# A one-token attention decode kernel: one head in each of six groups scored by a multiply and a reduce, the last group of heads scored on TensorE

## The chip, the cores and the metric

The kernel runs on one core of one Trainium2 chip. The metric is the device time of one execution in microseconds (us), as the median of several executions. The kernel before takes 87.77 us (median of 6 runs, 87.69 to 87.98). Profile times are of one profiled execution each, counted from the start of its span.

## The reference, cut to what matters

The input is one token (a row of 512). Attention and a feed-forward part both read its normalised form, and both are added to it.

```python
W = min(4096, max(256, Sk // 4))                      # 1024 keys of 4096
q = (x @ wq).reshape(B, Sq, 32, 128)                  # 32 heads of 128
k = k_cache[:, :, Sk - W:, :];  v = v_cache[:, :, Sk - W:, :]
scores = einsum("bhqd,bhkd->bhqk", q, k) * (128 ** -0.5)
o = einsum("bhqk,bhkd->bhqd", softmax(scores), v)
attn = o.reshape(B, Sq, 4096) @ wo
ffn  = (relu(xn @ w1 + b1) ** 2) @ w2 + b2
out  = x + attn + ffn
```

Nearly all of it is loading: 1024 keys and values of 32 heads, and four weight matrices, 27.99 MB in all.

## The kernel before

The heads are handled in eight groups of four. All large loads go through one queue, in a fixed order; five K blocks and four V blocks have room, so later ones wait until an earlier group has used its buffer.

```python
DMA_STREAM = ("wq0a", "k0", "wq0b", "wq1", "k1", "v0", "k2", "wq2", "w1", "k3", "wq3", "v1", "k4", "wo0", "v2", "k5", "w2a",
              "w2b", "wo1", "v3", "k6", "wo2", "k7", "v4", "wo3", "v5", "wo4", "v6", "wo5", "v7", "wo6", "wo7")
```

The scores of a head come from VectorE: 1024 keys lie as 128 partitions by J = 8 columns of 128 numbers. For each column, one fused instruction multiplies by the broadcast query and sums.

```python
for j in range(J):
    ins = E.tensor_tensor_reduce(
        out=ttr_views[junk_par][:, j, :], in0=KB[:, (h // G % NKSLOT) * G + h % G, j * DH:(j + 1) * DH],
        in1=qbc[:, di % NQBC, hh * DH:(hh + 1) * DH], scale=1.0, scalar=0.0,
        op0=ALU.mult, op1=ALU.add, accum_out=ScS[:, h, j:j + 1])
```

Then follow, per group, a maximum, the exponentials (ScalarE), the sum and the division (which gives `Pn`), P·V on TensorE, and the output product with `wo`, also on TensorE, summed up in one bank over all heads:

```python
for hh in range(G):                                   # emit_wo, for group g
    h = g * G + hh
    ins = E.matmul(FIN[0:1, 0:NOUT], lhsT=OTsb[:, h:h + 1], rhs=WoB[:, h, :], start=False, stop=(h == H - 1))
```

So the last thing that can happen is: the last V block (v7) and the last output weights (wo6, wo7) land, P·V of group 7, eight output matmuls, one copy, one store.

## Time and profile before

| What | Value | Where read |
|---|---|---|
| time, median | 87.77 us | the runs |
| span of the profiled execution | 85.9 us | page |
| VectorE busy | 66.5 us, 77% | page, part 1 |
| DMA engines 90% busy or more | 4 to about 75 us (the prediction read 2 to about 73) | page, part 2 |
| TensorE waits for v7 until | 78.75 us | timeline |
| ... for output weights until | 80.11 us | timeline |
| last eight output matmuls | 3.57 us | timeline |

The end of the chain of waits of the kernel before (start, us, what):

```profile
67.36 12.62 DMA WoB<-in_A_wo_dram
80.11 3.59 PE pb L770 x8
83.72 0.68 DVE finsb L806
```

Its timeline (start, us, engine, line, operation; in brackets the idle time before it and what ended that):

```profile
76.64 0.19 DVE L736 TENSOR_TENSOR Pn<-Ex,rden 128x32 bf16<-128x32 f32 x1
...
78.75 0.99 PE L752 MATMUL pb<-Pn,VB 128*128 128x1 bf16 x32 [0.57 <-DMA VB<-in_A_v_cache_dram]
...
80.11 3.57 PE L770 MATMUL pb<-WoB,OTsb 128*1 128x512 bf16 x8 [0.37 <-DMA WoB<-in_A_wo_dram]
```

Group 7's softmax is ready at 76.83 us (76.64 + 0.19). P·V then waits for the last V block until 78.75, and the output matmuls wait for their weights until 80.11. The loads end last, VectorE about 2 us before them.

The groups of VectorE's fused score instruction and its accumulator read (busy us, mean ns):

```profile
L667 DVE CUSTOM_DVE_ANT_0 ttrjunk<-KB,qbc 128x128 bf16<-128x128 bf16 x256 | 55.9, 279 | 2.6 <-ACT qbc L525 2.6
L667 DVE DVE_READ_ACCUMULATOR2_ANT ScS<- 128x1 f32 x256 | 19.3, 75 | 0.0
```

These 512 instructions are most of VectorE's 575. They overlap; in the timeline one fused instruction starts every 0.2125 us, so a head takes 8 x 0.2125 = 1.70 us.

### The profile page before, as it was taken

How to read it: one execution, taken by the hardware profiler on the slowest of the kernel's cores; microseconds unless marked ns; L12 is line 12 of the kernel's file. 1: busy time of each engine (PE TensorE's matmuls, PEld its weight loads, DVE VectorE, ACT ScalarE, POOL GpSimd, SP SyncE). 2: the span in 40 equal slices, each digit the busy share in tenths (PEclk: the TensorE clock that was granted, in tenths of full speed). 3: DMA queues.
4: the chain of work that ended last, by engine and by line, in shares of the span. 5: the costliest groups of instructions: out<-in, count | busy, mean ns of one | idle time of the engine just before them, and what ended most of it. 6: DMA issues, size and time to landing. Idle time of an engine off the chain costs nothing.

```text
span 85.9 us, 1607 instructions
## 1 busy us (share of the span) xinstructions
PE 50.1 (58%) x422; PEld 23.8 (28%) x424; DVE 66.5 (77%) x575; ACT 18.6 (22%) x84; POOL 1.5 (2%) x12
## 2 busy tenths in 40 slices
PE   0018769300269799596341119999415959677890
PEld 0002122000253395224240103245114252533210
DVE  0760799999998599999899999989999999310002
ACT  2370222205002250028006000400320060320000
POOL 6000000000000000000000000000000000000000
PEclk9999999999999999999999999999995555555555
DMA  0899999999999999999999999999999999971000
GB/s 2 293 394 372 387 387 385 386 386 391 390 387 386 381 386 387 376 368 385 385 358 344 348 379 387 370 376 388 370 381 367 379 364 383 365 246 41 15 0 0
DMA packets 17265, 28.09 MB, mean 327 GB/s; under 512 B 516, under 2 KB 7015, under 8 KB 17256
## 3 DMA queue, kind: packets, MB, share of 16 engines
q1 hardware_dynamic: 17252, 27.99, 91.6%
q8 instruction: 3, 0.05, 0.2%
q14 instruction: 6, 0.05, 0.2%
q10 hardware_dynamic: 4, 0.00, 0.0%
HBM read 27.99 MB, written 0.00 MB: 326 GB/s over the span
## 4 chain that ended last, share of the span: by engine, by line
DVE 40%; DMA 33%; PE 18%; ACT 3%; issue 3%; SPq 1%; DVEq 0%
DVE ttrjunk L667 30%; DMA VB<-in_A_v_cache_dram 17%; DMA WoB<-in_A_wo_dram 15%; PE pb L517 10%; PE pb L770 4%; PE pb L752 2%; DMA xrow<-in_A_x_dram 2%; DVE ScS L667 1%; ACT qbc L525 1%; ACT Ex L720 1%; SPq L285 1%; DVE gmx L695 1%; PE pb L688 1%; DVE finsb L806 1%; DVE st L375 1%
## 5 line engine op out<-in xcount | busy, mean ns | idle before, releaser
L667 DVE CUSTOM_DVE_ANT_0 ttrjunk<-KB,qbc 128x128 bf16<-128x128 bf16 x256 | 55.9, 279 | 2.6 <-ACT qbc L525 2.6
L667 DVE DVE_READ_ACCUMULATOR2_ANT ScS<- 128x1 f32 x256 | 19.3, 75 | 0.0
L517 PE MATMUL pb<-WqB,XnRep 128*128 128x512 bf16 x30 | 13.8, 631 | 2.8 <-DMA WqB<-in_A_wq_dram 1.4
L720 ACT ACTIVATE Ex<-ScS,nb 128x8 f32<-128x8 f32 x32 | 9.2, 289 | 25.7 <-DVE nb L710 25.7
L770 PE MATMUL pb<-WoB,OTsb 128*1 128x512 bf16 x32 | 12.1, 532 | 0.7 <-DMA WoB<-in_A_wo_dram 0.7
L752 PE MATMUL pb<-Pn,VB 128*128 128x1 bf16 x256 | 8.0, 165 | 5.1 <-DMA VB<-in_A_v_cache_dram 3.2
L752 PEld LDWEIGHTS pb<-Pn,VB 128*128 128x128 bf16 x256 | 7.4, 103 | 6.7 <-DMA VB<-in_A_v_cache_dram 2.8
L728 PE MATMUL pb<-rs,ones_f 128*128 128x4 f32 x16 | 4.5, 352 | 8.1 <-ACT Ex L720 4.8
L525 ACT ACTIVATE qbc<-pb 128x512 bf16<-128x512 f32 x8 | 4.8, 597 | 16.2 <-PE pb L517 16.2
L517 PEld LDWEIGHTS pb<-WqB,XnRep 128*128 128x128 bf16 x32 | 4.0, 137 | 10.4 <-issue 6.1
L728 PEld LDWEIGHTS pb<-rs,ones_f 128*128 128x128 f32 x16 | 3.8, 295 | 10.3 <-ACT Ex L720 5.1
L806 DVE CAST finsb<-pb 1x512 bf16<-1x512 f32 x1 | 0.7, 679 | 6.9 <-PE pb L770 6.9
L720 ACT ACTIVATION_READ_ACCUMULATOR Ex<-ScS,nb 128x1 f32 x32 | 6.0, 187 | 0.0
L704 PE MATMUL pb<-dgall,ones_bf 4*128 4x4 bf16 x8 | 1.4, 181 | 7.5 <-DVE dgall L697 7.5
L464 PE MATMUL pb<-W2B,hT 128*1 128x512 bf16 (+1 forms) x11 | 4.9, 627 | 0.0
L759 ACT ACTIVATE OTsb<-pb 128x4 bf16<-128x4 f32 x8 | 1.3, 165 | 16.3 <-PE pb L752 16.3
L688 PE MATMUL pb<-ident_bf,m 128*4 128x128 bf16 x8 | 2.1, 265 | 3.9 <-DVE m L679 3.1
L770 PEld LDWEIGHTS pb<-WoB,OTsb 128*1 128x1 bf16 x32 | 2.8, 98 | 5.7 <-issue 3.6
L704 PEld LDWEIGHTS pb<-dgall,ones_bf 4*128 4x128 bf16 x8 | 0.8, 98 | 10.5 <-DVE dgall L697 8.4
L414 PE MATMUL pb<-ones_bf,xnrow 1*128 1x1 bf16 x4 | 0.3, 165 | 5.6 <-DVE xnrow L404 5.6
L695 DVE TENSOR_REDUCE gmx<-pb 4x1 f32<-4x128 bf16 x8 | 2.2, 275 | 1.6 <-PE pb L688 1.6
L734 DVE RECIPROCAL rden<-pb 128x4 f32<-128x4 f32 x8 | 1.4, 174 | 2.2 <-PE pb L728 2.0
(45 smaller groups left out, 26.3 us busy)
## 6 DMA issues: line engine op xcount, KB each, us to landing
KB<-in_A_k_cache_dram SPq DMA_DIRECT2D x8, 1024.0 KB, 12.9
VB<-in_A_v_cache_dram SPq DMA_DIRECT2D x8, 1024.0 KB, 14.0
WoB<-in_A_wo_dram SPq DMA_DIRECT2D x8, 512.0 KB, 12.7
WqB<-in_A_wq_dram SPq DMA_DIRECT2D x3, 1024.0 KB, 15.0
W1B<-in_B_w_dram SPq DMA_DIRECT2D x1, 1376.0 KB, 15.5
W2B<-in_B_w_dram SPq DMA_DIRECT2D x1, 1280.0 KB, 12.9
WqB<-in_A_wq_dram SPq DMA_DIRECT2D x2, 512.0 KB, 5.4
W2B<-in_B_w_dram SPq DMA_DIRECT2D x1, 96.0 KB, 14.8
```

What stands on the lines that cost most here:

```text
L464: ins = E.matmul(FIN[0:1, 0:NOUT], lhsT=hT[0:cw, c:c + 1], rhs=W2B[0:cw, c, :], start=False, stop=False)
L517: ins = E.matmul(QBB[di % 2][:, 0:QBCW], lhsT=XnRep[:, kc, :], rhs=WqB[:, kc, g * QBCW:(g + 1) * QBCW], start=(kc == 0), stop=(kc == KC - 1))
L525: return K.E.activation(out=qbc[:, di % NQBC, :], in_=QBB[di % 2][:, 0:QBCW], func=ACT.Copy)
L667: ins = E.tensor_tensor_reduce(out=ttr_views[junk_par][:, j, :], in0=KB[:, (h // G % NKSLOT) * G + h % G, j * DH:(j + 1) * DH], in1=qbc[:, ...
L688: return K.E.matmul(hlpbf[0:G, TB_C0:TB_C0 + P], lhsT=m1[:, gs], rhs=ident_bf[:, :], start=True, stop=True, is_transpose=True)
L695: i1 = E.tensor_reduce(out=gmx[0:G, g:g + 1], in_=hlpbf[0:G, TB_C0:TB_C0 + P], axis=AX.X, op=ALU.max)
L704: return K.E.matmul(hlp[:, B_C0:B_C0 + G], lhsT=ones_bf[0:G, :], rhs=dgall[0:G, g, :], start=True, stop=True)
L720: ins = E.activation(out=Ex[:, h, :], in_=srcs[hh], func=ACT.Exp, bias=nb[:, h:h + 1], scale=SCALE, accum_out=rs[:, h:h + 1])
L728: return K.E.matmul(hlp[:, D_C0:D_C0 + G], lhsT=ones_f[:, :], rhs=rs[:, gs], start=True, stop=True)
L752: ins = E.matmul(hlp[:, OT_C0 + hh:OT_C0 + hh + 1], lhsT=VB[:, vh, j * DH:(j + 1) * DH], rhs=Pn[:, h, j:j + 1], start=(j == 0), stop=(j == ...
L770: ins = E.matmul(FIN[0:1, 0:NOUT], lhsT=OTsb[:, h:h + 1], rhs=WoB[:, h, :], start=False, stop=(h == H - 1))
L806: return K.E.tensor_copy(out=finsb[0:1, :], in_=FIN[0:1, 0:NOUT])
```

## The change

The intent is to relieve VectorE. In groups 0 to 5 one head each (3, 7, 11, 15, 19, 23) is scored by one multiply over all 1024 elements and one reduce, instead of eight fused instructions. Group 7's four heads are scored on TensorE: K is transposed there, ScalarE copies it out of PSUM, and TensorE multiplies it with the query. The diff, cut to its core:

```diff
+MIXED_PE_HEADS = {7: 4}
+TT_HEADS = (3, 7, 11, 15, 19, 23)
...
+    pe_heads = [h for h in range(H) if (h % G) >= G - n_pe_in_group[h // G]]
+    dve_heads = [h for h in range(H) if (h % G) < G - n_pe_in_group[h // G]]
...
+                    if h in TT_HEADS:
+                        K.sync(E.tensor_tensor(
+                            out=ttr_views[junk_par],
+                            in0=KB[:, (h // G % NKSLOT) * G + h % G, :].rearrange("p (j d) -> p j d", j=J),
+                            in1=qbc[:, di % NQBC, hh * DH:(hh + 1) * DH].unsqueeze(1).to_broadcast([P, J, DH]),
+                            op=ALU.mult))
+                        return E.tensor_reduce(out=ScS[:, h, :], in_=ttr_views[junk_par], axis=AX.X, op=ALU.add)
...
+            for p in plist:
+                make_pair_tasks(p)          # TensorE transposes, ScalarE copies
+            sdeps = ["ktc%d" % p for p in plist] + ["qTc%d" % g] + bank_free_deps
...
```

## The prediction

> **What bounds the kernel now.** The load stream. The page's 40 slices show the 16 DMA engines at 90% or more from 2 to about 73 us, and 27.99 MB moved; the stretch table gives 360 to 388 GB/s between 9 and 75 us. The chain of waits ends: V load 51.0 to 65.2, output-weight load 67.4 to 80.0, eight output matmuls 80.1 to 83.7 (3.6 us), copy 0.68, output DMA. VectorE is 77% busy and fills 40% of the chain, but the timeline shows its last score at 72.7 and the last weights (Pn) of group 7 at 76.8, while the last V block lands at about 78.7 and the output weights at 80.0. So VectorE has about 2 us of slack. Loads are issued back to back from 20 to 71.8 us; buffers come free earlier (the last V load is issued at 65.95, its releaser ends at about 60.1).
>
> **What the change does.**
> 1. Six heads (one in each of groups 0 to 5) swap eight fused multiply-reduces, 0.2125 us apart = 1.70 us per head, for one multiply of 1024 bf16 elements and one reduce. [...] From the trace's reduce (512 bf16: 674 ns) I estimate 1.2 us for the reduce[...]. With a wait between: about 1.9 us, 0.2 us *slower* per head, about +1.2 us of VectorE in all (at worst +4.5).
> 2. Group 7 leaves VectorE: -4 x 1.70 = -6.8 us. TensorE gets 32 transposes, 32 score matmuls and 16 small query matmuls, and loses four 512-wide ones; ScalarE gets four PSUM copies of 1024 (estimated about 1 us each, from 0.60 us for 512) and loses one of 0.60.
>
> VectorE net: some 2 to 6 us less busy (66.5 to about 61-63).
>
> **How much is on the critical path.** Almost none: bytes, load order and buffers are unchanged, so the last load still lands at about 80 us, followed by the same eight matmuls, copy and store.
>
> One real chance of gain: the TensorE clock. The last eight matmuls run 0.44 us apart; six of the same shape at 57.7 us ran 0.24 us apart. The stretch table puts the clock drop near 64 us, after 3 us of little TensorE work. [...] Group 7's transposes would run at about 62 to 66, in that hole. If the clock then stays up to the end, the last eight matmuls take 1.9 instead of 3.6 us: -1.7 us. I give that one in three.
>
> **Prediction:** 87.3 us, range 86.0 to 88.2. Faster by over 2%: 0.14; within 2%: 0.80; slower: 0.06.
>
> **What would show it.** Right: DMA slices unchanged, last output weights landing at 79.5 to 80.5, chain ending in DMA then output matmuls; VectorE busy 60 to 63; pair multiply+reduce about 1.9 us; Pn of group 7 ready several us before the last V. The clock question: spacing of the last eight matmuls, 0.24 or 0.44.
>
> **What would make it wrong.** VectorE slower in groups 0 to 5, starving the load queue; the in-order TensorE or ScalarE stalling on the new transposes or copies and pushing P·V past the load end; the slow trickle of the last loads between 75 and 80 us (138 GB/s) changing in length; the clock staying up (faster).

## More of the kernel before

The page of the kernel before, parts 1 to 3 (busy time by engine; the span in 40 slices of 2.15 us; the DMA queues with packets, MB, and share of the 16 engines' time). PE is TensorE's matmuls, PEld its weight loads, DVE VectorE, ACT ScalarE, POOL GpSimd:

```profile
span 85.9 us, 1607 instructions
...
PE 50.1 (58%) x422; PEld 23.8 (28%) x424; DVE 66.5 (77%) x575; ACT 18.6 (22%) x84; POOL 1.5 (2%) x12
...
DMA  0899999999999999999999999999999999971000
GB/s 2 293 394 372 387 387 385 386 386 391 390 387 386 381 386 387 376 368 385 385 358 344 348 379 387 370 376 388 370 381 367 379 364 383 365 246 41 15 0 0
...
q1 hardware_dynamic: 17252, 27.99, 91.6%
q8 instruction: 3, 0.05, 0.2%
q14 instruction: 6, 0.05, 0.2%
```

Two things are to be seen. The load stream is full almost to the end, but it does not stop at once: after 365 GB/s come 246, 41 and 15, so a small remainder dribbles in for about 6 us. And beside the kernel's own queue (q1) there are two queues called "instruction", with nine packets in all.

## The result, and the profile after

The changed kernel takes 86.43 us (median of 7 runs, 86.18 to 86.50). Executions over 1.5% slower than the fastest of the same kernel are left out of the means. The ratio to the kernel before is 0.9848, 95% interval 0.9836 to 0.9859. (A ratio is the mean time of one kernel's fast runs over that of the other's of the same rounds, so it is not quite the ratio of the medians.) The gain of 1.3 us is within the predicted range, but nearly three times the 0.47 us that was forecast.

The same parts of the page after (slices of 2.11 us):

```profile
span 84.3 us, 1614 instructions
...
PE 51.3 (61%) x499; PEld 26.1 (31%) x500; DVE 61.1 (73%) x428; ACT 21.6 (26%) x87; POOL 1.5 (2%) x12
...
DMA  0899999999999999999999999999999999995000
GB/s 2 290 389 370 386 387 386 387 388 387 392 388 387 385 389 387 386 364 383 388 368 349 330 363 388 378 371 383 384 367 381 365 382 368 381 359 176 23 0 0
...
q1 hardware_dynamic: 17252, 27.99, 93.5%
q8 instruction: 4, 0.07, 0.3%
q14 instruction: 4, 0.03, 0.1%
```

The kernel's own loads are the same: 17252 packets, 27.99 MB. VectorE is 5.4 us less busy. The remainder at the end is shorter, and the instruction packets have changed: q14 (8 KB a packet) fell from 6 to 4, q8 (16 KB a packet) rose from 3 to 4. TensorE's program grew from 870 to 1023 instructions, so q8 is most likely TensorE's.

The end of the chain of waits, and the timeline there:

```profile
65.17 11.86 DMA VB<-in_A_v_cache_dram
77.16 1.01 PE pb L747 x32
78.45 3.58 PE pb L765 x8
82.06 0.68 DVE finsb L801
```

```profile
75.21 0.19 DVE L731 TENSOR_TENSOR Pn<-Ex,rden 128x32 bf16<-128x32 f32 x1
...
77.16 0.99 PE L747 MATMUL pb<-Pn,VB 128*128 128x1 bf16 x32 [0.42 <-DMA VB<-in_A_v_cache_dram]
...
78.45 3.57 PE L765 MATMUL pb<-WoB,OTsb 128*1 128x512 bf16 x8 [0.29 <-ACT OTsb L754]
```

P·V of group 7 still waits for the last V block: 77.16 instead of 78.75 us. The eight output matmuls start at 78.45 instead of 80.11, 1.66 us earlier, and take the same 3.57 us. The span shrank by 1.67 us (85.9 to 84.3 rounded; 1.67 from the trace's own figures). So all the gain arises before the last load's end, and the question is why the same bytes, in the same order, arrive earlier. (The eight matmuls now wait for ScalarE's `OTsb`, which follows P·V of the last V block; wo6 had landed just before, at 78.32.)

The time fell by less than the span, 1.3 against 1.67 us. In every run of the changed kernel, and of e4 below, which has the same VectorE program, the time is 2.1 to 2.3 us longer than the span; in every run of the other kernels whose span is on record it is 1.7 to 1.9 us longer. Only the traces of these two hold one more packet of 8 KB on q14 after the span's end (at 85.9 us; the page does not count it). That this packet, one more fetch of instructions, costs the missing 0.3 us is likely, but was not tested.

The trace holds, for every load, the time at which each of its 16 DMA engines reported its part. The following is worked out from these times (not a view of the profile): the median of the 16, how far the second-last and the last engine were behind that median, and when the last landed.

```
                    before                          after
load     median  2nd-last  last   landed   median  2nd-last  last   landed
k3        28.54    +0.42  +1.87    30.41    28.56    +0.15  +0.88    29.44
k7        58.80    +1.49  +2.77    61.57    58.77    +1.66  +2.93    61.70
v4        61.54    +1.51  +3.68    65.22    61.51    +1.63  +2.91    64.41
v6        69.88    +1.52  +4.00    73.88    69.94    +1.60  +2.88    72.82
v7        74.11    +1.53  +4.50    78.61    74.08    +1.58  +2.94    77.03
wo6       75.62    +1.45  +4.36    79.98    75.59    +1.53  +2.72    78.32
wo7       76.99    +1.42  +4.33    81.31    77.06    +1.40  +2.59    79.65
instruction packets on q14, start us:
before   15.3  28.9  46.2  49.9  61.2  73.2        after   15.1  36.0  52.5  54.6
```

The median engine is just as far in both kernels (wo7: 76.99 and 77.06 us). Only the last engine differs: 4.33 us behind before, 2.59 after. A load counts as landed when all 16 have reported (P·V of group 7 began at 78.75 us before and 77.16 after, just behind the last report for v7 at 78.61 and 77.03, not behind the median's at 74.11 and 74.08), so this one engine sets the end. Its lag grows in steps of 0.4 to 1.0 us, and the steps stand at the instruction packets: in the kernel before the lag goes from +0.85 to +1.87 in the load being moved at 28.9 us, from +2.77 to +3.68 at 61.2, from +4.00 to +4.71 (wo5, not shown above) at 73.2.

That gives two theories.

- **Theory A.** One of the 16 DMA engines also fetches VectorE's instructions, in packets of 8 KB. Each fetch sets it back by up to 1 us. Its share of every load comes later, and with it the end of the kernel. The change gains because VectorE's compiled program is 150 instructions shorter (603 to 453).
- **Theory B.** The gain comes from the relief of VectorE, or from moving group 7 off it: it works less, so something that waits for it comes sooner.

### The profile page after: what moved, and what is told of

It is laid out like the page before. It is cut to its first block, busy times and chain, and to the rows that moved or that the text cites. A ratio compares the mean times of both kernels' runs of the same rounds, so it can differ in the third digit from the quotient of the medians.

```text
span 84.3 us, 1614 instructions
## 1 busy us (share of the span) xinstructions
PE 51.3 (61%) x499; PEld 26.1 (31%) x500; DVE 61.1 (73%) x428; ACT 21.6 (26%) x87; POOL 1.5 (2%) x12
## 3 DMA queue, kind: packets, MB, share of 16 engines
q1 hardware_dynamic: 17252, 27.99, 93.5%
HBM read 27.99 MB, written 0.00 MB: 332 GB/s over the span
## 4 chain that ended last, share of the span: by engine, by line
DVE 51%; DMA 30%; PE 13%; issue 2%; ACT 1%
DVE ttrjunk L630 32%; DMA KB<-in_A_k_cache_dram 15%; DMA VB<-in_A_v_cache_dram 14%; PE pb L522 6%; DVE ScS L628 6%; PE pb L765 4%; DVE ttrjunk L623 3%; DMA xrow<-in_A_x_dram 2%; DVE ScS L630 2%; PE pb L747 1%; DVE gmx L690 1%; DVE finsb L801 1%; DVE st L379 1%; DVE dgall L692 1%; DVE XnRep L427 1%
## 5 line engine op out<-in xcount | busy, mean ns | idle before, releaser
L630 DVE CUSTOM_DVE_ANT_0 ttrjunk<-KB,qbc 128x128 bf16<-128x128 bf16 x176 | 38.5, 283 | 3.3 <-ACT qbc L530 2.6
L522 PE MATMUL pb<-WqB,XnRep 128*128 128x512 bf16 x27 | 12.4, 630 | 2.5 <-DMA WqB<-in_A_wq_dram 1.3
L630 DVE DVE_READ_ACCUMULATOR2_ANT ScS<- 128x1 f32 x176 | 13.8, 79 | 0.0
L715 ACT ACTIVATE Ex<-ScS,nb 128x8 f32<-128x8 f32 x28 | 8.1, 289 | 16.8 <-DVE nb L705 16.7
L628 DVE TENSOR_REDUCE ScS<-ttrjunk 128x8 f32<-128x1024 bf16 x6 | 7.3, 1220 | 0.2
L522 PEld LDWEIGHTS pb<-WqB,XnRep 128*128 128x128 bf16 x28 | 3.4, 136 | 9.3 <-issue 5.0
L715 ACT ACTIVATION_READ_ACCUMULATOR Ex<-ScS,nb 128x1 f32 x28 | 5.2, 187 | 0.0
L683 PEld LDWEIGHTS pb<-ident_bf,m 128*4 128x4 bf16 x8 | 0.6, 81 | 14.3 <-DVE m L673 12.7
L623 DVE TENSOR_TENSOR ttrjunk<-KB,qbc 128x1024 bf16<-128x1024 bf16 x6 | 4.1, 681 | 0.0
L577 ACT ACTIVATE KTs<-pb 128x1024 bf16<-128x1024 bf16 x4 | 3.7, 1009 | 0.0
```

What stands on the lines that cost most here:

```text
L522: ins = E.matmul(QBB[di % 2][:, 0:QBCW], lhsT=XnRep[:, kc, :], rhs=WqB[:, kc, g * QBCW:(g + 1) * QBCW], start=(kc == 0), stop=(kc == KC - 1))
L577: ins = E.activation(out=KTs[:, slots[hi], :, :], in_=banks[hi][:, :].rearrange("d (j p) -> d j p", j=J), func=ACT.Copy)
L623: K.sync(E.tensor_tensor(out=ttr_views[junk_par], in0=KB[:, (h // G % NKSLOT) * G + h % G, :].rearrange("p (j d) -> p j d", j=J), in1=qbc[ ...
L628: return E.tensor_reduce(out=ScS[:, h, :], in_=ttr_views[junk_par], axis=AX.X, op=ALU.add)
L630: ins = E.tensor_tensor_reduce(out=ttr_views[junk_par][:, j, :], in0=KB[:, (h // G % NKSLOT) * G + h % G, j * DH:(j + 1) * DH], in1=qbc[:, ...
L683: return K.E.matmul(hlpbf[0:G, TB_C0:TB_C0 + P], lhsT=m1[:, gs], rhs=ident_bf[:, :], start=True, stop=True, is_transpose=True)
```

## The experiments

Eleven runs of eight kernels. In each call the kernel before ran beside them on the same chip, with medians of 87.79, 87.66 and 87.86 us (the last a single run, on another chip). Program lengths are those of the compiled programs, in instructions of 64 bytes (VectorE's 603 are 38,592 bytes). The diffs are shortened, and the remarks behind # are added here.

### Each half of the change alone

```diff
-MIXED_PE_HEADS = {7: 4}
+MIXED_PE_HEADS = {}                  # e1_tt_only
```

> Six heads as multiply+reduce, group 7 still on VectorE. VectorE program 603 -> 515 instructions of 64 B, VectorE work about 1.2 us more. Theory A (the last load is late because one DMA engine also fetches VectorE's instructions, 8 KB = 128 instructions at a time, about 1 us of lag each): one fetch fewer (4 instead of 5 in the stream), lag of the slowest DMA engine 3.3 to 3.9 us instead of 4.3, time 87.0 to 87.5. Theory B (the gain is VectorE or group-7 relief): no gain, 87.8 to 88.5.

```diff
-TT_HEADS = (3, 7, 11, 15, 19, 23)
+TT_HEADS = ()                        # e2_g7_only
```

> Group 7 on TensorE, all other heads as before. VectorE program 603 -> 540 instructions. Theory A: one fetch fewer, lag 3.3 to 3.9 us, time 87.0 to 87.5, and this part alone gives less than half of the whole gain. Theory B (VectorE or group-7 relief): the whole gain or more, 85.5 to 86.5.

Measured: e1_tt_only 86.97 us (ratio 0.9907, interval 0.9891 to 0.9923); e2_g7_only 86.89 us (0.9888, 0.9869 to 0.9907). Both beat the expected 87.0 to 87.5 by a hair. The last engine's lag in wo7 was 3.59 and 3.47 us, inside the expected range, and each had five packets on q14, one fewer than before. One part of the expectation was missed: e2 was to give less than half of the whole gain, and each half gave more than half of it (0.8 and 0.9 of 1.3 us). Of the 1.67 us by which the span shrank each half gave 0.76, nearly all together; in the time the whole change shows less, because of the stretch after the span's end, described above.

The first of the two speaks plainly against Theory B: VectorE was busier than before (66.8 us to 66.5), nothing had left it, and the kernel was still 0.8 us faster. Its line of the page, and its timeline at the end, which also shows what group 7's move adds:

```profile
PE 50.0 (59%) x424; PEld 23.8 (28%) x424; DVE 66.8 (78%) x491; ACT 18.5 (22%) x84; POOL 1.5 (2%) x12
```

```profile
78.10 0.19 DVE L731 TENSOR_TENSOR Pn<-Ex,rden 128x32 bf16<-128x32 f32 x1
78.35 1.01 PE L747 MATMUL pb<-Pn,VB 128*128 128x1 bf16 x32 [0.50 <-DVE Pn L731]
79.36 3.57 PE L765 MATMUL pb<-WoB,OTsb 128*1 128x512 bf16 x8
```

Here P·V waited for VectorE's `Pn` (78.29 us), no longer for v7 (landed at 77.90). With group 7 still on VectorE, a still earlier load end could not have been used. The move of group 7 is worth its own fetch, and it clears the way for the other.

### The instructions put back, without work

```diff
                             op0=ALU.mult, op1=ALU.add, accum_out=ScS[:, h, j:j + 1])
+                        E.wait_ge(dma_sems['d_x'], 16)       # e3_dve_waits: changed kernel plus
+                        E.wait_ge(dma_sems['d_wq0a'], 16)    # satisfied waits, 453 -> 629 instructions
```

> The changed kernel with 176 extra already satisfied waits in VectorE's program between the fused multiply-reduces (629 instructions), computing the same. Theory A: five fetches again, lag 4 us or more, time back at 87.5 to 88.2. Theory B: VectorE still ends long before the last load, so 86.3 to 86.7.

Measured: 87.88 us, ratio to the kernel before 1.0007 (0.9989 to 1.0026). The whole gain is gone. Its queues, and its timeline:

```profile
q8 instruction: 4, 0.07, 0.3%
q14 instruction: 6, 0.05, 0.2%
```

```profile
79.06 0.99 PE L749 MATMUL pb<-Pn,VB 128*128 128x1 bf16 x32 [0.81 <-DMA VB<-in_A_v_cache_dram]
...
80.42 3.57 PE L767 MATMUL pb<-WoB,OTsb 128*1 128x512 bf16 x8 [0.37 <-DMA WoB<-in_A_wo_dram]
```

VectorE's work is that of the changed kernel (61.3 us busy, 428 counted instructions); only its program is longer. q14 is back at six packets, the last engine is 4.58 us behind in wo7, and both TensorE steps wait for loads again. The median engine finished wo7 at 77.04 us, as in the other two kernels, so the waits did not delay the loads as a whole. The length of VectorE's program alone moved the time by 1.45 us (86.43 to 87.88), and the span by 2.0 us (84.27 to 86.24), as much as the lag grew.

### The same test on an idle engine

```diff
             run_engine("POOL", E)
+            for _ in range(1280):                            # e4_pool_waits: 29 -> 670 instructions
+                E.wait_ge(dma_sems['d_x'], 16)               # (two waits make one instruction)
```

> The changed kernel with 641 extra satisfied waits at the end of GpSimd's program, which does nothing else by then. Theory A: 4 to 5 more 8 KB fetches in the first half; if they fall on the DMA engine that fetches for VectorE the last load is 4 us or more later (90 us); if on another one, that one becomes the slowest with 3 to 5 us of lag (86.5 to 88.5). Theory B: no change, 86.3 to 86.6.

Measured: 86.49 us, ratio 0.9854 (0.9836 to 0.9872), as the changed kernel. q14 had nine packets, five more for 641 more instructions, so a packet of 8 KB holds about 128:

```profile
q14 instruction: 9, 0.07, 0.2%
```

The lags, sorted load by load, rise in two separate series: one by about 1 us at VectorE's later fetches (35.9 and 54.5 us), as in the changed kernel, the other by about 0.3 to 0.7 us at each of GpSimd's five (10.6 to 56.0 us). At wo7 the last two engines are 2.83 and 2.46 us behind (2.59 and 1.40 without the waits). So GpSimd's fetches most likely fall on another DMA engine than VectorE's, and that one ends about level with it or just behind. The landing times do not name the engines, so this is read from the steps. The time is what Theory B expected, and 0.01 us below Theory A's range of 86.5 to 88.5; the lag of 3 to 5 us that Theory A expected was not reached at wo7. The run does not separate the two by its time. It shows that a fetch does not always cost the same.

### VectorE relieved, with as many instructions

```diff
-        in0=KB[:, ..., j * DH:(j + 1) * DH], in1=qbc[:, ..., hh * DH:(hh + 1) * DH], ...
+        in0=KB[:, ..., j * DH:j * DH + DH // 2], in1=qbc[:, ..., hh * DH:hh * DH + DH // 2], ...   # e5_half_width
```

> The kernel before, with each fused multiply-reduce over 64 of its 128 columns: wrong result on purpose, same number of instructions (603), VectorE busy some 10 to 17 us less. Theory A (fetches on one DMA engine): five fetches as before, lag 4 us or more, time 87.4 to 88.1. Theory B (VectorE relief): 86.4 or less.

Measured: 87.86 us, ratio 1.0026 (1.0011 to 1.0041).

```profile
PE 49.8 (58%) x424; PEld 23.2 (27%) x424; DVE 50.1 (58%) x575; ACT 18.8 (22%) x84; POOL 1.5 (2%) x12
q14 instruction: 6, 0.05, 0.2%
```

VectorE's busy time fell from 66.5 to 50.1 us, three times what the change saves, and nothing was gained. q14 has six packets, the lag in wo7 is 4.53 us. Theory B falls. (The kernel leaves out half of every score sum on purpose. The comparison with the reference nevertheless called it correct, so it is too coarse to see the scores; this run is no proof of a right result.)

### Fewer instructions still

```diff
-TT_HEADS = (3, 7, 11, 15, 19, 23)
+TT_HEADS = tuple(range(28))          # e6_all_tt: changed kernel, all its VectorE heads; 145 instructions
```

> The changed kernel with all 28 VectorE heads as multiply+reduce: VectorE program 453 -> 145 instructions, VectorE work about 4.4 us more (22 heads x 0.2). Theory A: at most one fetch in the stream on the slow DMA engine, its lag about 1.0; the engines that fetch for TensorE (lag about 1.5) are then the last ones, so the last output weights land 1.0 to 1.3 us earlier: 85.0 to 85.6. Theory B: slower than 86.4 or the same.

Measured: 90.39 us, ratio 1.0311 (1.0289 to 1.0334): slower than before. Half of the expectation held. With two packets on q14, the last engine was only 1.34 us behind, and the output weights landed at 77.16 (wo6) and 78.50 us (wo7), earlier than in any kernel above. (The lag of about 1.5 us that the expectation gives to TensorE's fetches: the second-last engine went from +0.42 to +1.55 us after q8's packet at 33.6 us in the kernel before, and from +0.17 to +1.50 after the one at 37.3 us in the changed kernel.) Theory B's words for this run ("slower than 86.4 or the same") fit the time. But the time was lost elsewhere, as the timeline shows:

```profile
74.01 1.22 DVE L628 TENSOR_REDUCE ScS<-ttrjunk 128x8 f32<-128x1024 bf16 x1
...
83.34 1.01 PE L747 MATMUL pb<-Pn,VB 128*128 128x1 bf16 x32
...
84.62 1.87 PE L765 MATMUL pb<-WoB,OTsb 128*1 128x512 bf16 x4 [0.26 <-ACT OTsb L754]
```

VectorE's last score reduce ended at 75.23 us; the softmax and P·V of two groups come after it, and the load end no longer matters. A head now costs 0.68 + 1.22 us and two gaps, 1.97 us, against 1.70. For 22 heads that is about 6 us, as an estimate from these durations. VectorE also stood still for 5.9 us before `nb`, the step just before the exponentials (1.8 in the changed kernel), waiting for TensorE, whose order of work differs here because the kernel's own list scheduler plans each of these heads at 2.4 us. How the delay divides between the two was not tried.

Two heads in one multiply and one reduce keep VectorE's time and still save the instructions:

```diff
-for hh in range(nd):                                  # eight fused instructions, or multiply + reduce
+for hh in range(0, nd, 2):                            # e7_pair_g7: one task each for
+    E.tensor_tensor(out=ttrjunk[:, u % 2, :, :, :],   # the multiply of two heads (2048 elements)
+        in0=KB[:, ks:ks + 2, :]..., in1=qbc[..., hh * DH:(hh + 2) * DH]... .to_broadcast([P, 2, J, DH]), op=ALU.mult)
+    E.tensor_reduce(out=ScS[:, h:h + 2, :], in_=ttrjunk[:, u % 2, :, :, :], axis=AX.X, op=ALU.add)
```

> As the run with all heads as multiply+reduce, but two heads in one multiply and one reduce (2048 elements): VectorE program 118 instructions, VectorE work about 1.75 us per head, as with the fused instruction. Theory A: 85.0 to 85.6. Theory B: about 86.4.

Measured: 84.91 us (6 runs, 84.68 to 85.46), ratio 0.9702 (0.9673 to 0.9732). It beats both kernels: 3% under the kernel before, and just under the expected 85.0 to 85.6. Its times lie in two groups, 84.7 to 84.95 and 85.45 us. The profiled run was of the slower group, and in it the last engine was already 2.37 us behind at the second load, before any fetch in the stream.

> The same kernel as e7_pair_g7, whose times fell in two groups (84.7 to 84.95 and 85.45); the profile was of 85.45 and showed one DMA engine 2.4 us behind from the second load on, before any fetch in the stream. Theory A: if this profile is of the faster group, that early lag is absent, and the last engine is 1.3 to 1.6 us behind at the end instead of 2.0.

Measured: 84.94 us, of the faster group. The early lag was +0.48, and at wo7 +1.64. The expected 1.3 to 1.6 was missed by a hair. What holds an engine up at the start of some executions was not found. The slower profile is 0.5 us longer (85.45 against 84.94), and its lag of 2.01 at wo7 is the remainder of the early 2.37, not the mark of a fetch. The queues and the end of this run:

```profile
q8 instruction: 4, 0.07, 0.3%
q14 instruction: 2, 0.02, 0.1%
```

```profile
73.82 0.19 DVE L723 TENSOR_TENSOR Pn<-Ex,rden 128x32 bf16<-128x32 f32 x1
76.08 0.99 PE L739 MATMUL pb<-Pn,VB 128*128 128x1 bf16 x32 [0.72 <-DMA VB<-in_A_v_cache_dram]
...
77.46 3.43 PE L757 MATMUL pb<-WoB,OTsb 128*1 128x512 bf16 x8 [0.38 <-DMA WoB<-in_A_wo_dram]
```

`Pn` is ready 2 us before the V block, and both TensorE steps wait for loads, now at 76.08 and 77.46 us. VectorE's busy time (59.8 us) is close to the changed kernel's 61.1.

The same pairs for all 32 heads, with nothing moved to TensorE (`MIXED_PE_HEADS = {}`):

> Pairs of heads on VectorE for all 32 heads, nothing moved to TensorE: VectorE program 119 instructions, TensorE program 871 as before (one fetch of 16 KB fewer than the changed kernel), VectorE as busy as before. Theory A: the load ends 1.2 to 1.6 us earlier than in the changed kernel, but group 7's softmax on VectorE ends at about 76 to 77 and may now be the later one: 85.0 to 86.3, in any case below the kernel before by more than 1.4 us. Theory B: about as the kernel before, 87.7.

Measured: median 87.32 us, but in two groups, 85.37 and 85.63 against four runs of 87.28 to 87.57. The faster group lies where Theory A put it, 85.0 to 86.3; the median does not, and is nearer to Theory B's 87.7. Two more looks at it:

> The same kernel as e8_pair_all, whose times fell in two groups (85.4 to 85.6, 87.3 to 87.6) with the profile in the faster one. If this profile is of the slower group: theory A expects the loads to end as early as in the faster one (lag 1.3 to 2.0) and something after or beside them to be late; if instead the lag is 3.5 us or more, the number of instructions does not set it and theory A falls.

> As e8_again: a second look at the same kernel, to catch the slower group.

Measured: 85.67 and 85.63 us, both of the faster group, as the first profile was. The slower group was never caught in a profile, and its cause stays open. In the three profiles the last engine was 1.60, 1.42 and 2.43 us behind in wo7, and the chain of waits before the last matmuls ran through VectorE, ScalarE and TensorE, not through a load: with group 7 on VectorE, compute has become the limit. Without the change's second half the shorter program pays less, and less reliably.

### All runs in one table

"VectorE fetches" are the packets on q14 less one that stands in every kernel (of the two at 46.2 and 49.9 us before, and of those at 52.5 and 54.6 after, only one goes with a step of the last engine, +1.81 to +2.77 and +1.89 to +2.85 us; whose the other is was not shown) and, in e4, less the five that came with GpSimd's instructions. The lag is that of the last DMA engine in wo7.

| kernel | VectorE program | VectorE busy, us | VectorE fetches | lag, us | median time, us |
|---|---|---|---|---|---|
| before | 603 | 66.5 | 5 | 4.33 | 87.75 |
| e5_half_width | 603 | 50.1 | 5 | 4.53 | 87.86 |
| e3_dve_waits | 629 | 61.3 | 5 | 4.58 | 87.88 |
| e2_g7_only | 540 | 60.2 | 4 | 3.47 | 86.89 |
| e1_tt_only | 515 | 66.8 | 4 | 3.59 | 86.97 |
| after | 453 | 61.1 | 3 | 2.59 | 86.43 |
| e4_pool_waits | 453 | 61.0 | 3 | 2.83 | 86.49 |
| e7_pair_g7 | 118 | 59.8 | 1 | 2.01, 1.64 | 84.91 |
| e8_pair_all | 119 | 66.0 | 1 | 1.60, 1.42, 2.43 | two groups |
| e6_all_tt | 145 | 63.6 | 1 | 1.34 | 90.39 |

Down to e7 the time follows the number of fetches, and not the busy time. In e8 and e6 the lag is as small, but compute ends last.

## Why the prediction was right or wrong, point by point

- **"The load stream" bounds the kernel; VectorE has about 2 us of slack.** Right. Halving VectorE's score width (e5) took 16 us off its busy time and changed nothing.
- **Reduce 1.2 us, about 1.9 us per head, slower than the fused form.** Right. The reduce was worked out from the trace before (674 ns for 512 elements); the multiply's part of the 1.9 us, and the worst case of +4.5 us, were the author's estimate, read from no trace. The changed kernel's groups (busy us, mean ns):

```profile
L628 DVE TENSOR_REDUCE ScS<-ttrjunk 128x8 f32<-128x1024 bf16 x6 | 7.3, 1220 | 0.2
L623 DVE TENSOR_TENSOR ttrjunk<-KB,qbc 128x1024 bf16<-128x1024 bf16 x6 | 4.1, 681 | 0.0
```

  From 1024 to 2048 elements (e7_again) the multiply grew from 681 to 1214 ns and the reduce from 1220 to 2279, so 0.52 and 1.03 ns for each further element.
- **VectorE busy 61 to 63 us.** Right: 61.1. ScalarE's four copies at about 1 us each: 1.009 us.
- **"Bytes, load order and buffers are unchanged, so the last load still lands at about 80 us."** This is the step that failed. It took equal loads to mean an equal end. The wo6 block, which it had at 80.0, landed at 78.32 us (expected 79.5 to 80.5), and the last block, wo7, at 79.65 instead of 81.31. Left out was a load that the kernel does not issue: the fetching of its instructions (q14 and q8: 0.10 MB before), by the same DMA engines and with VectorE's fetches all on one of them, as the steps of the lag suggest. Removing 150 instructions removed two fetches and 1.74 us of the last engine's lag. The profile before had shown it: the q14 line, and the remainder of 41 and 15 GB/s after 77 us. The prediction named that remainder as something that might change in length, without asking what makes it.
- **The DMA slices would be unchanged.** Wrong only at the end: the tail reads 359, 176, 23 instead of 365, 246, 41, 15 GB/s.
- **The TensorE clock might stay up to the end (one in three), for -1.7 us.** It did not: the last eight matmuls took 3.57 us both times, and the clock in the stretch tables is 0.50 after 75 us in both. The rows of the stretch from 60 to 70 us (busy us of PE, PEld, DVE, ACT, POOL; clock; DMA share; GB/s), before and then after, show the transposes' work:

```profile
60.00:70.00 10.00, 5.24 (x68) 2.62 (x65) 9.93 (x94) 2.23 (x15) 0.00 (x0) 0.71 1.06 374
```

```profile
60.00:70.00 10.00, 6.90 (x110) 4.87 (x110) 6.64 (x58) 6.19 (x21) 0.00 (x0) 0.82 1.07 375
```

  The granted clock was 1.00 from 60 to 64 us and 0.50 from 66 to 70 in the kernel before, 1.00 from 65 to 66 and 0.50 from 70 to 75 after; the clock records of the two traces put the drop in this stretch at 64.2 and 66.3 us. That the transposes would hold the clock up was the author's estimate; no run here shows that they did. The mean clock of the span differed from run to run of one and the same kernel (0.654 to 0.881 before, 0.654 to 0.777 after), so two profiles are too few to tell. Nor does it go with the time: the changed kernel's runs, with those means, had times within 0.4%. A saving of 1.7 us was expected from this possibility, and one of 1.67 us of span came from another cause: without a look at the spacing of the matmuls the two would be easily confused.
- **`Pn` of group 7 "ready several us before the last V".** Wrong in size: 75.40 against 77.03 us (landing), 1.6 us, as little as before. Both moved forward.
- **The size.** The forecast of -0.47 us was one third of a clock gain plus nothing from the loads. The loads gave all of it. That the time still fell inside the predicted range was luck: the range left room for the clock, which gave nothing, and for the last loads' trickle, which was named without a size or a cause.

What is shown and what is inferred: that VectorE's program length sets the load end is shown by e3 (added instructions) and e5 (removed work), and agrees with e1, e2 and e7. That VectorE's fetches all fall on one engine, which is then the last, and GpSimd's on another, is inferred from lags growing by steps at the fetches; the trace's landing times do not name the engine. Why a packet that itself takes about 0.35 us (0.353 to 0.388 on q14 in the kernel before) sets the engine back by up to 1 us was not tried.

## What to carry to other kernels

When a kernel is bound by its loads, look at how the stream ends, not only at how full it is: if most engines are done and one is not, find what that one does besides. Here it fetched instructions, by all signs, so the instruction count of an engine off the critical path cost about 0.7 to 0.9 us of time for each VectorE fetch of about 128 instructions (from e1, e2, e3 and e7); fewer and larger instructions were worth it even where each took longer, as long as compute stayed behind the loads (e7, 3% faster than before), and no longer where it did not (e6, 3% slower). To test such a cause, add empty instructions and remove work with the count held fixed; the two together decide it. And compare the time with the span: what comes after the last instruction is in the time, but not on the page.
